# Retention and a gated feed-forward: the gates of 256 tokens by seven quarter products

## The chip, the cores and the metric

One core of one Trainium2 chip. The metric is device time in microseconds (us). The kernel works in bf16 with fp32 sums, on five engines: TensorE (PE), VectorE (DVE), ScalarE (ACT), GpSimd (POOL) and SyncE (SP, which issues DMAs). They run side by side and wait for each other by semaphores.

## The reference

```python
def _attn_ref(q, k, v):                       # (8, 8, 576, 64) each
    scores = scale * np.matmul(q, k.transpose(0, 1, 3, 2))
    gamma = 1.0 - 2.0 ** (-5.0 - np.arange(H))
    Dmat = np.where(rel >= 0, gamma[:, None, None] ** rel[None], 0.0)   # rel = pos_i - pos_j
    return np.matmul(scores * Dmat[None], v)

def _moe_ref(x, w_gate, w_val, w_out):        # x: 4608 tokens x 512; w: 512 x 1536, 1536 x 512
    gate = 1.0 / (1.0 + np.exp(-(x @ w_gate)))
    return (gate * (x @ w_val)) @ w_out
```

The tokens of the feed-forward are the retention's outputs, all heads of one position side by side.

## The kernel before

The retention is worked out in chunks of 64 positions with a running state, so that a "chunk group" makes, for two steps of 128 tokens, the masked scores (`row`), their products with v (`val`), the products with the old state, and the new state's share (`new`). The results stand transposed in `xT`, feature rows by token columns, which the feed-forward reads as the moving operand of its matmuls.

The feed-forward goes over the tokens in blocks: tokens 0 to 511, then `BLOCKS`: two blocks of 256 (512 and 768), then blocks of 512 from 1024 on. Of each block it makes the gates (`g`: products with `w_gate`, then a sigmoid on ACT), the values (`v`: products with `w_val`, multiplied into the gates on DVE, the result is `gv`), and the output products (`op`, with `w_out`).

The blocks of 512 tokens use seven products in the place of eight (Strassen's scheme in Winograd's form): a unit of four feature chunks by all 512 tokens is cut in quarters, and sums of quarters of the weights (`w_sums`, in `wgt_sb` for gates, `wvt` for values), of x (`xsum`) and of the products give the result. `quarter_units` makes one product at a time: `quarter("g", u, i)` is product i of gate unit u, short `gui`: g15 is product 5 of unit 1. Products 1, 6, 7 and 4 gather in the tile `gatea`, 5 and 3 in `gatee`, and 2 is added to a copy of `gatea` in `gateg`; ACT copies what is needed between (`gu`, `gs`), DVE adds, ACT takes the sigmoids. Before the change the two blocks of 256 tokens don't use this: `h_units` makes, for pairs of feature chunks, eight gate products and eight value products of 256 columns in turn (`h_g`, `h_v`), and `op_units` the output products.

There are eight PSUM banks: `tr`, `pv`, `st` one each, `qk` two, `ffn` three, used in a ring (`Ring`), so that a product's tile waits for the reader of the tile before it in its bank.

The order is written out by hand: each generator yields after a piece, and the loop over `BLOCKS` puts between the pieces what tables say. `SUMS_AT` has entries as 0.3:g00p: in block 0 of `BLOCKS` (tokens 512 to 767) at piece 3, sum 0 of gate unit 0 on POOL (p) or DVE (v); o are sums of `w_out` (`wt_sb`), w of the values' weights, c casts of the next chunks' inputs, t transposes on PE. `PAIRS_AT` says at which pieces the chunk groups of the next tokens stand. `CUTS` and `OP_CUTS` say how many 512-column products are made in two halves of 256 columns.

Of the kernel before, what the change touches and what calls it, by code (L numbers as in the profile page):

```python
# [9 lines left out]
FP32 = mybir.dt.float32  # L10
BF16 = mybir.dt.bfloat16
AF = mybir.ActivationFunctionType
ALU = mybir.AluOpType
# [3 lines left out]
def kernel(  # L17
# [19 lines left out]
    nc = tc.nc  # L37
# [4 lines left out]
    P = 128  # L42
    M = H // 2
    NC = (S + P - 1) // P
    NKC = DM // P
    NFC = DFF // P
# [43 lines left out]
    SUMS = 8  # L90
# [785 lines left out]
    def h_units(gvs, fcs, t0, n):  # L876

        for fc in fcs[::2]:
            gv_tile(gvs, t0, fc)
            both = made[t0, fc // 4][:, fc % 4:fc % 4 + 2, 0:n]  # L880
            for what, w_sb in (("g", wg_sb), ("v", wv_sb)):
# [9 lines left out]
                yield 8 * n  # L891

    def gv_unit(t0, u):

        return gv_pool.tile([P, 4, 512], BF16, tag="gv", name=f"gv_{t0}_{u}")
# [91 lines left out]

    def first_x_sum(i, eng):

        if 0 not in turned_x:  # L990
            turned_x[0] = [ld_pool.tile([P, 2, 2, 256], BF16, tag="xsum", name=f"xsum_0_{i}", bufs=SLOTS["xsum"])
                           for i in range(2)]
        t1, t2, t3, t4 = (turned_x[0][i][:, j] for i in range(2) for j in range(2))
        b11, b12, b21, b22 = (xT(slice(r, r + 2), slice(c, c + 256)) for r in (0, 2) for c in (0, 256))
        to, a, b = ((t1, b12, b11), (t3, b22, b12), (t2, b22, t1), (t4, b21, t2))[i]
        eng.tensor_tensor(out=to, in0=a, in1=b, op=ALU.subtract)
# [4 lines left out]

    def quarter_units(gvs, t0):

        BANKS = {("g", 0): [(tr_psum, "tr"), (pv_psum, "pv"), (qk_psum, "qk")],
                 ("g", 1): [(qk_psum, "qk"), (ffn_psum, "ffn"), (st_psum, "st")],
                 ("g", 2): [(pv_psum, "pv"), (st_psum, "st"), (st_psum, "st") if thirds(t0) else (tr_psum, "tr")],
                 ("w", 0): [(ffn_psum, "ffn"), (qk_psum, "qk"), (ffn_psum, "ffn")],
                 ("w", 1): [(ffn_psum, "ffn"), (ffn_psum, "ffn"), (ffn_psum, "ffn")],
                 ("w", 2): [(qk_psum, "qk"), (qk_psum, "qk"), (tr_psum, "tr")]}
        waiting = []  # L1010

# [3 lines left out]

        def bank(kind, u, i):
# [3 lines left out]
            return pool.tile([P, 2, 256], FP32, tag=tag, name=f"{name}_{t0}_{u}", **more)  # L1020

        def keep(kind, u, name, ps, eng=on_act):
            t = sum_tile([P, 2, 256], FP32, f"{kind}{name}_{t0}_{u}")
            eng(out=t, in_=ps)
            return t

        def right(i):
            x = xT(ALL, slice(t0, t0 + 512))
            t = turned_x[t0] if i > 3 else None
            return {1: lambda: x[:, 0:2, 0:256], 2: lambda: x[:, 2:4, 0:256], 3: lambda: x[:, 2:4, 256:512],  # L1030
                    4: lambda: t[1][:, 1], 5: lambda: t[0][:, 0], 6: lambda: t[0][:, 1], 7: lambda: t[1][:, 0]}[i]()

# [18 lines left out]
        def quarter(kind, u, i, by=nc.gpsimd):  # L1051

            me = of.setdefault((kind, u), {})
            if i == 1:
                gv_tile(gvs, t0, 4 * u)
                me["a"] = bank(kind, u, 0)
            if i == 5:
                me["e"] = bank(kind, u, 2)
            a, e = me.get("a"), me.get("e")
            product(kind, u, i, {1: a, 6: a, 7: a, 4: a, 5: e, 3: e, 2: me.get("g")}[i], i in (1, 5))  # L1060
            behind_copy = i in (1, 5) and (t0 == BLOCKS[2][0] and i == 1 or (kind, u) == ("w", 0))
            if not behind_copy and (kind, u, i) != ("g", 1, 5):
                settle()

            def leaves(r, h, src, eng=nc.vector, parts=1):
                for n in range(parts):
                    part = slice(2 * n // parts, 2 * (n + 1) // parts)
                    to = made[t0, u][:, 2 * r:2 * r + 2, h * 256:(h + 1) * 256][:, part]
                    if kind == "g":
                        nc.scalar.activation(out=to, in_=src[:, part], func=AF.Sigmoid)  # L1070
                    else:
                        eng.tensor_tensor(out=to, in0=to, in1=src[:, part], op=ALU.mult)  # L1072

            if i == 1:
                me["g"] = bank(kind, u, 1)
                nc.scalar.copy(out=me["g"], in_=a)  # L1076
            elif i == 2:
                leaves(0, 0, me["g"])
            elif i == 5:
                me["s5"] = keep(kind, u, "s5", e, on_dve if t0 == BLOCKS[2][0] and (kind, u) in KEEP_DVE else on_act)  # L1080
            elif i == 6:
                me["u2"] = keep(kind, u, "u2", a)
            elif i == 3:
                nc.vector.tensor_tensor(out=me["u2"], in0=e, in1=me["u2"], op=ALU.add)  # L1084
# [8 lines left out]
            return 4 * 256  # L1093

        H_CUTS = 4

        def value(fc):
# [13 lines left out]
            return 4 * 512  # L1111

        return quarter, value

# [180 lines left out]

    OP_CUTS = (6, 11, 0, 0)

# [59 lines left out]

    CUTS = 60
    cut = []
# [110 lines left out]
    for i in range(2):  # L1470
        first_x_sum(i, nc.vector)
    first_sum(sbd[3], "share_1", on_act)
# [16 lines left out]

    step(units, 1)  # L1490
    first_x_sum(2, nc.vector)
    step(units, 1)
    first_x_sum(3, nc.vector)
    step(units, 2)
# [46 lines left out]
    def op_first(fcs, nbs, opps):  # L1541
        for fc in fcs:
            for nb in nbs:
# [51 lines left out]

    SUMS_AT = ("0.0:c03p 0.1:f00p 0.3:g00p 0.3:w10v 0.3:w11v 0.6:t01p 0.7:o10p 0.8:c02v "
# [3 lines left out]
               "2.22:o02p 2.39:o12v 3.2:w20v 3.2:w21v 3.3:w23v 3.9:w22v").split()  # L1600
    sums_at = {}
    for x in SUMS_AT:
# [5 lines left out]
            w_sums(k, i, u, eng))  # L1608
    PAIRS_AT = ((0, 10), (0, 11), (1, 10), (1, 0))
    paired = 0  # L1610
# [4 lines left out]
    for w, (t0, n) in enumerate(BLOCKS):  # L1615
# [13 lines left out]
        while w > 1 and (not twos and valued < last or twos and twos[-1][0][-1] < last):  # L1629
            vals = list(range((twos[-1][0][-1] if twos else valued) + 1, at))  # L1630
            twos.append((vals, list(range(at, min(at + 2, NS)))))
            at = min(at + 2, NS)
        for i, cols in enumerate(ffn_units(t0, n, nxt)):
            for x in sums_at.get((w, i), ()):
                x()
# [20 lines left out]
        assert not twos  # L1656
        assert w != 1 or paired == len(PAIRS_AT)
        while len(pending) > (w == 1):
            pending.pop(0)()
# [31 lines left out]
```

## Time and profile before

| | |
|---|---|
| median of 3 runs | 303.66 us (303.56 to 304.35) |
| the profiled execution | 303.61 us |
| its span, first instruction to last | 302.0 us |
| PE busy | 295.4 us (98%), 4430 matmuls recorded |
| DVE, ACT, POOL busy | 230.1, 204.6, 224.9 us (76%, 68%, 74%) |
| granted TensorE clock | 1.0 |

The times of the trace count from the start of the span; the 1.6 us between span and run lie outside it. A row of the timeline has start, length and instruction, with xN where N alike follow each other; the length of a row of matmuls includes the way of the last one through the array, so paces are read from start to start. A few matmul records are missing.

### The profile page before, as it was taken

Reading aid. Unit: us, or ns where it says so; the run is one execution under the profiler, and the core shown is the slowest. Engines: PE = TensorE matmul, PEld = TensorE weight load, DVE = VectorE, ACT = ScalarE, POOL = GpSimd, SP = SyncE. Lnnn points to the kernel's source line nnn. Section 1 sums busy time; section 2 is a strip of 40 time slices with the busy share of each in tenths; the row PEclk is TensorE's granted clock in tenths of the full one; section 3 lists DMA queues with packets and bytes.
Section 4 is the critical chain, followed back from the end, with each engine's and each line's share of the span. In section 5 each row is a group of like instructions: output and inputs, shape, how many; then the busy total and the mean of one; then the engine's idle time right before and its main releaser. Section 6 shows DMA issues by size and latency. Waiting matters only on the chain.

```text
span 302.0 us, 10689 instructions
## 1 busy us (share of the span) xinstructions
PE 295.4 (98%) x4430; PEld 250.4 (83%) x4437; DVE 230.1 (76%) x439; ACT 204.6 (68%) x414; POOL 224.9 (74%) x253
## 2 busy tenths in 40 slices
PE   8999999999999999999999999999999999999994
PEld 3687876978868888888888888888888888888883
DVE  5967995686886998789748974896489848935793
ACT  6764574345369747985798589857985698559830
POOL 5775754846479898978997898789978947860780
PEclk9999999999999999999999999999999999999999
DMA  7999999979899979897759967976793165004013
GB/s 205 309 339 398 362 345 239 209 155 210 174 197 222 248 176 225 186 221 211 143 114 200 250 143 155 194 207 146 128 204 127 37 111 205 4 2 139 3 36 104
DMA packets 146464, 54.99 MB, mean 182 GB/s; under 512 B 124400, under 2 KB 139760, under 8 KB 146416
## 3 DMA queue, kind: packets, MB, share of 16 engines
q1 hardware_dynamic: 145328, 53.59, 73.3%
q10 hardware_dynamic: 1088, 0.72, 0.8%
q8 instruction: 34, 0.56, 0.8%
q14 instruction: 14, 0.11, 0.1%
HBM read 37.75 MB, written 9.44 MB: 156 GB/s over the span
## 4 chain that ended last, share of the span: by engine, by line
PE 86%; DMA 7%; SPq 4%; POOL 1%; issue 0%; ACT 0%; DVE 0%
PE gatea L1045 12%; PE wa L1045 12%; PE qa L1172 11%; PE qe L1172 9%; PE gatee L1045 6%; PE we L1045 6%; PE h_v L885 4%; PE h_g L885 3%; PE op L1305 3%; DMA wv<-in_moe_w_val_dram 3%; PE op L1548 3%; PE gateg L1045 3%; PE wg L1045 3%; SPq L186 3%; DMA wg<-in_moe_w_gate_dram 2%; PE val L717 2%
## 5 line engine op out<-in xcount | busy, mean ns | idle before, releaser
L1045 PEld LDWEIGHTS <-wg_sb 128*128 128x128 bf16 x348 | 34.0, 98 | 4.2
L1072 POOL TENSOR_TENSOR gv<-gv,wu 128x512 bf16<-128x512 bf16 x20 | 23.5, 1174 | 16.1 <-DVE wu L1084 16.0
L1172 PEld LDWEIGHTS <-gsum 128*128 128x128 bf16 x312 | 29.9, 98 | 3.7
L1045 PEld LDWEIGHTS <-wv_sb 128*128 128x128 bf16 x296 | 29.0, 98 | 3.4
L429 POOL TENSOR_TENSOR qk<-q,qtab 128x512 bf16<-128x512 f32 x28 | 30.1, 1073 | 1.4 <-DMA q<-in_q_dram 1.4
L1084 DVE TENSOR_TENSOR gu<-gatee,gu 128x512 f32<-128x512 f32 x22 | 15.2, 690 | 19.4 <-ACT gateg L1076 10.2
L1045 PEld LDWEIGHTS <-wgt_sb 128*128 128x128 bf16 x264 | 25.8, 98 | 3.0
L942 POOL TENSOR_TENSOR gsum<-gsum,gv 128x256 bf16<-128x256 bf16 (+1 forms) x20 | 17.6, 891 | 14.4 <-DVE gsum L942 12.6
L1045 PE MATMUL gatea<-xsum,wg_sb 128*128 128x256 bf16 x172 | 25.6, 273 | 0.0
L1172 PEld LDWEIGHTS <-gv 128*128 128x128 bf16 x228 | 21.8, 98 | 2.7
L429 POOL TENSOR_TENSOR qk<-k,ktab 128x512 bf16<-128x512 f32 x11 | 12.1, 1097 | 13.9 <-DMA k<-in_k_dram 9.6
L1087 DVE TENSOR_TENSOR gs<-gatea,gs 128x512 f32<-128x512 f32 x22 | 15.1, 688 | 9.4 <-PE gatea L1045 9.3
L942 POOL TENSOR_TENSOR gsum<-gv,gsum 128x256 bf16<-128x256 bf16 (+1 forms) x24 | 21.9, 921 | 0.2
L703 DVE TENSOR_TENSOR pt<-row,tri 128x512 bf16<-128x512 f32 x30 | 19.2, 681 | 2.9 <-PE row L686 2.7
L442 POOL TENSOR_TENSOR v<-v,ktab 128x512 bf16<-128x512 f32 x19 | 20.9, 1100 | 0.0
L1045 PE MATMUL wa<-xsum,wv_sb 128*128 128x256 bf16 x136 | 20.4, 273 | 0.0
L658 ACT CAST sb<-s 128x512 bf16<-128x512 f32 (+1 forms) x26 | 14.3, 569 | 8.4 <-DVE s L828 8.3
L787 ACT CAST xT<-val 128x512 bf16<-128x512 f32 x26 | 14.7, 592 | 7.0 <-PE val L733 7.0
L942 DVE TENSOR_TENSOR gsum<-gv 128x512 bf16<-128x512 bf16 (+1 forms) x34 | 18.7, 576 | 0.0
L1045 PEld LDWEIGHTS <-wvt 128*128 128x128 bf16 x168 | 16.4, 98 | 1.9
L942 POOL TENSOR_TENSOR gsum<-gv 128x256 bf16<-128x256 bf16 (+1 forms) x20 | 17.6, 880 | 0.0
L1070 ACT ACTIVATE gv<-gu 128x512 bf16<-128x512 f32 x22 | 14.0, 638 | 5.2 <-DVE gu L1084 5.2
(210 smaller groups left out, 882.6 us busy)
## 6 DMA issues: line engine op xcount, KB each, us to landing
k<-in_k_dram SPq DMA_DIRECT2D x26, 256.0 KB, 3.8
q<-in_q_dram SPq DMA_DIRECT2D x26, 256.0 KB, 4.2
v<-in_v_dram SPq DMA_DIRECT2D x26, 256.0 KB, 4.6
out_dram<-ob SPq DMA_DIRECT2D x24, 256.0 KB, 2.8
wg<-in_moe_w_gate_dram SPq DMA_DIRECT2D x12, 256.0 KB, 5.3
wv<-in_moe_w_val_dram SPq DMA_DIRECT2D x12, 256.0 KB, 5.2
wo<-in_moe_w_out_dram SPq DMA_DIRECT2D x12, 256.0 KB, 5.3
v32p<-in_v_dram SPq DMA_DIRECT2D x6, 256.0 KB, 4.7
```

Source lines behind the costliest of these rows:

```text
L429: eng.tensor_tensor(out=to, in0=by_halves(loaded[s][1 - i]), in1=tab, op=ALU.mult)
L442: nc.gpsimd.tensor_tensor(out=natural["v", s], in0=loaded[s][2], in1=tab, op=ALU.mult)
L658: eng(out=both_steps["sb", b, c][:, js], in_=both_steps["s32", b, c][:, js])
L703: nc.vector.tensor_tensor(out=t[:, y, 0:n].rearrange("p i m t -> p (i m) t"), in0=rows_tile[ss[0]][y][:, 0:n].rearrange("p i m t -> p (i m ...
L787: nc.scalar.copy(out=to, in_=src)
L885: nc.tensor.matmul(ps[:, i], lhsT=w_sb[:, kc, (fc + i) * P:(fc + i + 1) * P], rhs=xT(kc, slice(t0, t0 + n)), start=(kc == 0), stop=(kc == ...
L942: eng.tensor_tensor(out=to, in0=a, in1=b, op=op)
L1045: nc.tensor.matmul(ps[:, f], lhsT=w[:, kc, f * P:(f + 1) * P], rhs=x[:, kc], start=(first and f == 0 and kc == 0), stop=(f == 1 and kc == ...
L1072: eng.tensor_tensor(out=to, in0=to, in1=src[:, part], op=ALU.mult)
L1084: nc.vector.tensor_tensor(out=me["u2"], in0=e, in1=me["u2"], op=ALU.add)
L1087: nc.vector.tensor_tensor(out=me["s5"], in0=a, in1=me["s5"], op=ALU.add)
L1172: nc.tensor.matmul(ps[:, b], lhsT=left(fp)[:, b * P:(b + 1) * P], rhs=right(fp), start=(first and fp == 0 and b == 0), stop=(fp == NFC // ...
```

## The change

The gates of tokens 768 to 1023 (the second block of 256) are made by seven quarter products of 128 columns each, as in the large blocks; the values stay plain products of 256 columns. `h_quarters` has the order of both in the table `SHORT`. Sums of x for that block are made by DVE ahead of it (`block_x_sum`). The sums of the gates' weights, which only tokens from 1024 on needed, are thus needed a block earlier and stand earlier in `SUMS_AT`: two go from POOL to DVE, two value sums from DVE to POOL. The chunk groups stand at other pieces. Halved products: 29 in place of 60 allowed in block 0 (48 were there), none in place of 17 in block 512's output products; matmuls in all stay at 4437.

```diff
+    SHORT = (("", "g01 g15 g11 v0", "g02 g05 g06 g16 g12", "g13 g03 g07 g17", "g21 v4 g04 g14 m", "v6 m m", "g26 v2 v8 g25", "g22", "m g27 g23", "V10", "m g24 m V11 m", ""),)
+
+    def h_quarters(gvs, t0, n):
+        quarter, _ = quarter_units(gvs, t0, n)
+        mults = []
+        for steps in SHORT[0]:
+            cols = 0
+            for x in steps.split():
+                if x == "m":
+                    quarter.settle()
+                    to, by = mults.pop(0)
+                    nc.vector.tensor_tensor(out=to, in0=to, in1=by, op=ALU.mult)
+                elif x[0] == "g":
+                    cols += quarter("g", int(x[1]), int(x[2]))
+                else:
...
+            yield cols
...
-    def first_x_sum(i, eng):
+    def block_x_sum(t0, n, i, eng):
...
-    def quarter_units(gvs, t0):
+    def quarter_units(gvs, t0, n=512):
+        m = n // 2
...
+        if n < 512:
+            BANKS["g", 0][2] = (st_psum, "st")
+            BANKS["g", 1][2] = (ffn_psum, "ffn")
...
-    OP_CUTS = (6, 11, 0, 0)
+    OP_CUTS = (0, 0, 0, 0)
...
-            yield from h_units(gvs, range(NFC), t0, n)
+            yield from h_quarters(gvs, t0, n) if t0 == BLOCKS[1][0] else h_units(gvs, range(NFC), t0, n)
...
-    CUTS = 60
+    CUTS = 29
...
-    SUMS_AT = ("0.0:c03p 0.1:f00p 0.3:g00p 0.3:w10v 0.3:w11v 0.6:t01p 0.7:o10p 0.8:c02v "
+    SUMS_AT = ("0.0:c03p 0.1:f00p 0.3:g00v 0.3:w10v 0.3:w11v 0.4:o10p 0.6:t01p 0.8:c02v 0.8:g01v 0.8:c05p "
...
-    PAIRS_AT = ((0, 10), (0, 11), (1, 10), (1, 0))
+    PAIRS_AT = ((0, 8), (0, 13), (1, 10), (1, 2))
...
+        X_SHORT = ('vvvv',)
+        if w == 1:
+            for i in range(4):
+                block_x_sum(t0, n, i, nc.vector if X_SHORT[0][i] == "v" else nc.gpsimd)
```

What this moves is seen at three places. The first is DVE behind the masks `pt` of the second chunk group of block 512 (`s` are the running states, `wt_sb` a sum of `w_out`, `h_v` the values of block 768). Before:

```order
L703 TENSOR_TENSOR pt_2_1619<-row_2_1_1536,tri_274 128x512
L830 COPY s32_2_0_1632<-new_2_0_1569 128x256
L828 TENSOR_TENSOR s32_2_0_1632<-s32_2_0_1632,new_2_1_1570 128x256
L828 TENSOR_TENSOR s32_2_1_1646<-s32_2_0_1632,new_2_0_1569 128x256
L828 TENSOR_TENSOR s32_2_1_1646<-s32_2_1_1646,new_2_1_1570 128x256
L324 TENSOR_TENSOR wt_sb_278<-wo_sb_277 128x512
L890 TENSOR_TENSOR gv_768_0_1661<-gv_768_0_1661,h_v_768_0_1673 128x2x256
```

And in the changed kernel, from the multiply of block 512's last values on:

```order
L890 TENSOR_TENSOR gv_512_2_1269<-gv_512_2_1269,h_v_512_10_1430 128x2x256
L365 TENSOR_TENSOR wg_sb_275<-wg_sb_275 128x2x256 x2
L703 TENSOR_TENSOR pt_2_1590<-row_2_0_1506,tri_274 128x512
L703 TENSOR_TENSOR pt_2_1590<-row_2_1_1507,tri_274 128x512
L830 COPY s32_2_0_1601<-new_2_0_1540 128x256
L828 TENSOR_TENSOR s32_2_0_1601<-s32_2_0_1601,new_2_1_1541 128x256
L365 TENSOR_TENSOR wg_sb_275<-wg_sb_275 128x2x256
L828 TENSOR_TENSOR s32_2_1_1613<-s32_2_0_1601,new_2_0_1540 128x256
L828 TENSOR_TENSOR s32_2_1_1613<-s32_2_1_1613,new_2_1_1541 128x256
L1023 TENSOR_TENSOR xsum_768_0_1628<-xT_768_1599 128x2x128
L1023 TENSOR_TENSOR xsum_768_1_1629<-xT_768_1599 128x2x128
```

Three gate sums (in place, in `wg_sb`) and the sums of x have come in; two more sums of x follow the last row shown, then the adds of the quarter products. The second place is ACT within the gates of block 768. Before:

```order
L888 ACTIVATE gv_0_1661<-h_g_0_1662 128x2x256
L888 ACTIVATE gv_0_1661<-h_g_2_1683 128x2x256
L888 ACTIVATE gv_1_1705<-h_g_4_1706 128x2x256
L888 ACTIVATE gv_1_1705<-h_g_6_1728 128x2x256
L888 ACTIVATE gv_2_1750<-h_g_8_1751 128x2x256
L888 ACTIVATE gv_2_1750<-h_g_10_1771 128x2x256
```

In the changed kernel, unit 2's part, which is the end of it:

```order
L1107 COPY gateg_2_1727<-gatea_2_1721 128x256
L1101 ACTIVATE gv_0_1634<-gatea_0_1635 128x2x128
L1101 ACTIVATE gv_1_1649<-gatea_1_1650 128x2x128
L1055 COPY gu_768_2_1766<-gatea_2_1721 128x256
L1055 COPY gs_768_2_1791<-gatee_2_1786 128x256
L1101 ACTIVATE gv_2_1720<-gateg_2_1727 128x2x128
L1101 ACTIVATE gv_2_1720<-gs_768_2_1791 128x2x128
L1101 ACTIVATE gv_2_1720<-gu_768_2_1766 128x2x128
L1101 ACTIVATE gv_2_1720<-gatea_2_1721 128x2x128
L787 CAST xT_2000<-val_0_1870 128x2x8x32
```

Six sigmoids have become nine copies and twelve sigmoids of half the width, and the last of them reads the bank that the next chunk group's `val` takes over. The third place is DVE in front of the first chunk group of block 512 (`T` is a turned input of that group):

```order
L890 TENSOR_TENSOR gv_512_0_1145<-gv_512_0_1145,h_v_512_2_1201 128x2x256
L365 TENSOR_TENSOR wgt_sb_279<-wg_sb_275 128x512
L365 TENSOR_TENSOR wvt_0_855<-wv_sb_276 128x512
L365 TENSOR_TENSOR wvt_1_856<-wvt_0_855,wv_sb_276 128x512
L890 TENSOR_TENSOR gv_512_1_1214<-gv_512_1_1214,h_v_512_4_1226 128x2x256
L632 COPY T_1_1246<-turn_1_1_1253 128x512
```

The gate sum in the second row is new here, where before the two `wvt` sums stood alone.

More of the change, by code (lines that the diff above doesn't have):

```diff
@@ L1014, in settle, with quarter_bank @@
                 waiting.pop(0)()
-        def bank(kind, u, i):
+        def quarter_bank(kind, u, i):
             pool, tag = BANKS[kind, u][i]
@@ L1065, in leaves @@
             def leaves(r, h, src, eng=nc.vector, parts=1):
-                for n in range(parts):
-                    part = slice(2 * n // parts, 2 * (n + 1) // parts)
-                    to = made[t0, u][:, 2 * r:2 * r + 2, h * 256:(h + 1) * 256][:, part]
+                for p in range(parts):
+                    part = slice(2 * p // parts, 2 * (p + 1) // parts)
+                    to = made[t0, u][:, 2 * r:2 * r + 2, h * m:(h + 1) * m][:, part]
                     if kind == "g":
@@ L1074, in quarter @@
             if i == 1:
-                me["g"] = bank(kind, u, 1)
+                me["g"] = quarter_bank(kind, u, 1)
                 nc.scalar.copy(out=me["g"], in_=a)
@@ L1092, in quarter @@
                 settle()
-            return 4 * 256
+            return 4 * m
         H_CUTS = 4
@@ L1111, in value @@
             return 4 * 512
+        quarter.settle = settle
         return quarter, value
@@ L1657 @@
         assert w != 1 or paired == len(PAIRS_AT)
+        assert not [x for x in sums_at if x[0] == w]
         while len(pending) > (w == 1):
```

47 lines of the change are left out of this document (29 added, 18 removed), and 3 rows, old and new, of the table SUMS_AT.

## The prediction

> **What bounds the kernel now.** I read the page first: its busy times, then the chain that ended last.
>
> ```profile
> PE 295.4 (98%) x4430; PEld 250.4 (83%) x4437; DVE 230.1 (76%) x439; ACT 204.6 (68%) x414; POOL 224.9 (74%) x253
> ...
> PE 86%; DMA 7%; SPq 4%; POOL 1%; issue 0%; ACT 0%; DVE 0%
> ```
>
> TensorE (PE) is the bound: 295.4 of 302.0 us, and 86% of the chain. Busy PE proves little where matmuls overlap, so I looked at starts. The timeline of PE, in the stretch that changes (start, us, instruction):
>
> ```profile
> 47.41 2.97 PE L1548 MATMUL op<-wo_sb,gv 128*128 128x512 bf16 x13 [0.16 <-issue]
> 50.21 0.61 PE L630 MATMUL turn<-ident,qk 128*128 128x128 bf16 x8
> ...
> 51.52 1.04 PE L885 MATMUL h_g<-xT,wg_sb 128*128 128x256 bf16 x8
> 52.40 1.04 PE L885 MATMUL h_v<-xT,wv_sb 128*128 128x256 bf16 x8
> 53.27 1.04 PE L885 MATMUL h_g<-xT,wg_sb 128*128 128x256 bf16 x8
> ...
> 57.64 0.61 PE L630 MATMUL turn<-ident,qk 128*128 128x128 bf16 x8
> 58.08 1.04 PE L885 MATMUL h_v<-xT,wv_sb 128*128 128x256 bf16 x8
> ```
>
> Start to start, eight products of 256 columns take 0.875 us (109 ns each), eight of 128 columns 0.44 to 0.45 (56 ns), thirteen of 512 columns 2.80 (215 ns). In all three the next group starts when the columns are through, and no other row of these stretches shows PE waiting. The later part of the same timeline:
>
> ```profile
> 65.90 0.32 PE L717 MATMUL val<-pt,v 64*64 64x64 bf16 x16
> ...
> 67.15 2.79 PE L1305 MATMUL op<-wo_sb,gv 128*128 128x512 bf16 x23
> 69.78 1.04 PE L885 MATMUL h_g<-xT,wg_sb 128*128 128x256 bf16 x8
> ...
> 79.50 0.34 PE L717 MATMUL val<-pt,v 64*64 64x64 bf16 x18
> ...
> 88.62 1.04 PE L1045 MATMUL gatea<-xT,wg_sb 128*128 128x256 bf16 x8
> ```
>
> A chunk group takes 1.25 us (65.90 to 67.15), and block 768's twelve groups fill 69.78 to 79.50 but for the last, with no idle time marked. So before has next to no PE wait here to remove: the change can win only columns, and loses whatever wait it makes.
>
> **PE's own work.** Removed: 48 gate products of 256 columns, 48 x 109 ns = 5.24 us. Added: 84 products of 128 columns (three units, seven products, four matmuls), 84 x 56 ns = 4.70 us. That is -0.54 us. Halving: 19 value and gate products in front and 17 output products of block 512 become whole; two halves are 2 x 109 = 218 ns, a whole one 215, so 36 x 3 ns = -0.11 us. The count of PE instructions stays equal (36 more, 36 fewer). Sum: **-0.65 us**.
>
> The eight turns each load their own weights, as the new products do; a load is listed longer than that pace:
>
> ```profile
> L630 PEld LDWEIGHTS <-qk 128*128 128x128 bf16 x24 | 1.6, 98 | 0.5
> ```
>
> 98 ns a load against 56 ns a product means that loads overlap each other, but eight in a row after long products is a short test, while the new gates run up to 36 in a row. I take 56 ns, the row of the same shape; the upper bound is a load's whole 98 ns, 84 x 42 = +3.5 us.
> The Trainium skill ("TensorE: Matmul & The Clock Gate", Back-to-back issue gap) speaks against this term: it states about 81 ns per matmul for a sustained stream of weight loads and 128-column matmuls, and 56 only for an isolated gap. By that figure the term would be 84 x 81 = 6.8 us, +1.56 instead of -0.54, an estimate; the trace's eight at 56 ns disagree as far as they go.
>
> **VectorE in front of the gates.** Quarter products need sums of x before the second of them (g15), so VectorE (DVE), free of it before, now stands in PE's way. Its rows after the chunk group at 65.90, and what a bf16 sum costs:
>
> ```profile
> 55.89 0.42 DVE L365 TENSOR_TENSOR wvt<-wv_sb 128x512 bf16<-128x512 bf16 x1
> 56.34 1.15 DVE L365 TENSOR_TENSOR wvt<-wvt,wv_sb 128x512 bf16<-128x512 bf16 x1
> 57.41 0.68 DVE L890 TENSOR_TENSOR gv<-gv,h_v 128x512 bf16<-128x512 bf16 x1
> ...
> 66.86 1.29 DVE L703 TENSOR_TENSOR pt<-row,tri 128x512 bf16<-128x512 f32 x2 [0.37 <-PE row L686]
> 68.06 0.41 DVE L830 COPY s<-new 128x256 f32<-128x256 f32 x1
> 68.51 1.40 DVE L828 TENSOR_TENSOR s<-s,new 128x256 f32<-128x256 f32 x3
> ```
>
> GpSimd (POOL) beside them:
>
> ```profile
> 56.09 1.12 POOL L429 TENSOR_TENSOR qk<-k,ktab 128x512 bf16<-128x512 f32 x1 [0.24 <-DMA k<-in_k_dram]
> ...
> 58.91 1.15 POOL L365 TENSOR_TENSOR wgt_sb<-wg_sb 128x512 bf16<-128x512 bf16 x1
> ...
> 68.67 1.04 POOL L429 TENSOR_TENSOR qk<-k,ktab 128x512 bf16<-128x512 f32 x1 [4.77 <-DMA k<-in_k_dram]
> 69.68 1.04 POOL L429 TENSOR_TENSOR qk<-q,qtab 128x512 bf16<-128x512 f32 x1
> ```
>
> The sum at 56.34 took 1.15 instead of 0.42 and ended at 57.49, just behind POOL's product, which ended at 57.21: a DVE sum of two SBUF tensors stands still while POOL works. The Trainium skill ("SBUF — State Buffer", SBUF: two separate sides) has this as an exclusive lock on a port pair that the two share, held for a whole instruction; the trace agrees (1.15 against 0.42 us), and the rule speaks against adding such sums to DVE.
>
> Let C be the start of the chunk group in front of block 768's gates. PE: 1.25 us of chunks, then 16 whole output products, 16 x 0.215 = 3.45, first gate product at C+4.70, g15 four products later at C+4.92. DVE: masks from C+0.96 (66.86 - 65.90), state sums until C+4.01 (68.51 + 1.40 = 69.91), one weight sum between them (0.42, or 1.15 beside POOL), then the first x sum of 256 columns, nearest row:
>
> ```profile
> L942 DVE TENSOR_TENSOR gsum<-gv 128x256 bf16<-128x256 bf16 x12 | 3.5, 333 | 0.0
> ```
>
> So the sum is there at C+4.01+0.42+0.33 = C+4.76 at best, and with POOL's products at 68.67 and 69.68 in the way at up to C+4.01+1.15+0.9 = C+6.0. In front of the masks DVE now also has h_v_10's multiply and two gate sums, 0.68 + 2 x 0.42 = 1.5 us that came earlier or later before. PE's wait: 0 to 1.1 us; I take **+0.4**, since the group and POOL's casts fall near each other.
> Farther in front, one gate sum (0.42 to 1.15 us) is queued ahead of h_v_4's multiply, which frees the bank of h_g_8. That multiply ended at 58.09 (57.41 + 0.68) and h_g_8 follows h_v_6 at 58.95, so 0.86 us covers it: a wait of 0 to 0.3. One output-weight sum comes ahead of the state that the second chunk group reads, at worst the 0.73 by which a stuck sum is longer than a free one. Both need POOL at the wrong moment: **+0.1**.
>
> **ScalarE within the gates.** Six sigmoids of 512 columns become nine copies and twelve sigmoids of 256. Rows by form, and the delay from PE:
>
> ```profile
> L888 ACT ACTIVATE gv<-h_g 128x512 bf16<-128x512 f32 x12 | 7.2, 597 | 11.6 <-PE h_g L885 11.6
> ...
> L1236 ACT COPY ob<-qa 128x256 f32<-128x256 f32 x12 | 3.9, 376 | 2.7 <-PE qa L1172 2.7
> ...
> L1444 ACT ACTIVATE gv<-hg 128x256 bf16<-128x256 f32 x4 | 1.4, 384 | 1.4 <-PE hg L1438 1.4
> ...
> 52.60 0.60 ACT L888 ACTIVATE gv<-h_g 128x512 bf16<-128x512 f32 x1 [0.29 <-PE h_g L885]
> ```
>
> That is 9 x 0.376 + 12 x 0.384 = 8.0 us for 3.6, in some 10 us of PE time: ScalarE (ACT) keeps up on average, so what counts is each turnaround. ACT starts 0.20 us after PE goes on (52.60 - 52.40), so a copy is done 0.58 us after its product. From unit 2's fifth product to its third lie two products of 4 x 56 ns, 0.45 us: a wait of 0.13. The last sigmoid frees the bank that the next chunk group writes first; between its product and that group lies one value product of 4 x 109 = 0.44 us against 0.20 + 0.384, and a VectorE sum of 0.33 with its sigmoid is queued before it: 0.1 to 0.3. Together 0 to 0.6, taken **+0.3**. The v2 and v8 products wait for multiplies of v0 and v4 on DVE, which two output-weight sums now precede; POOL mostly waits for loads there, so 0, at worst 0.5.
>
> **Moved for nothing.** Two gate sums leave POOL (1.15 us each, row at 58.91), and one value sum comes to it early; its casts there start by the loads (4.77 us of waiting at 68.67), so neither shortens nor delays them. A last value sum goes from DVE to POOL in block 1536, where POOL has this room:
>
> ```profile
> POOL gv L1072 <- DVE wu L1084: 16.0, 7, 7.1
> ```
>
> Without it, it would cost up to the 1.15. Earlier casts issue their loads and transposes on SyncE in the same order as before.
>
> **Sum:** -0.65 + 0.4 + 0.1 + 0.3 = +0.15 us on the profiled execution's 303.61 (span 302.0 and 1.6 around it), 303.8 us. The median of the three runs is 303.66, so the same to 0.05.
>
> **Rivals.** (A) No wait survives: the turnarounds overlap, DVE has its sums in time. Then 303.61 - 0.65 = 303.0. For it: DVE is idle a quarter of the span. Against: C+4.76 for C+4.92 leaves 0.16. (B) DVE becomes the bound ahead of the gates: each of the weight sums falls beside a POOL product, and g15 waits 1.1 us, h_g_8 and the chunk state 0.8 of their 1.0, with 0.3 behind: 303.61 - 0.65 + 2.2 = 305.2; half of the port losses give 304.5. It decides as slower once these waits pass 0.65 + 0.9 = 1.55 us. For it: seven more bf16 sums on DVE between 53 and 71 us. Against: POOL stood idle from 63.9 to 68.67. (C) The new products don't hold 56 ns, since a load of 98 ns shows through: up to 303.8 + 3.5 = 307.3. The product rows speak against it. By the sustained 81 ns of the Trainium skill ("TensorE: Matmul & The Clock Gate", Back-to-back issue gap) it would be 303.8 + 84 x 25 ns = 305.9, again an estimate. (D) The halved products were worth more than 3 ns each as fillers; 36 of them made whole move every later instruction by less than 0.11 us, so no case of its own.
>
> **How the numbers follow.** A measurement of this kernel can tell about 0.3%, 0.9 us, from no change: 302.75 to 304.57. Forecast 0.50 (0.47 within, 0.03 slower), A 0.20 (0.16 within, 0.04 faster, as it would need more than PE's columns), B 0.24 (0.22 slower, 0.02 within), C 0.06 slower. Faster 0.04, same 0.65, slower 0.31. The range goes from A's 303.0 less 0.1 to B's 305.2.
>
> **What would show it.** In the profile after: h_g's 48 rows for block 768 gone, 84 of 128 columns at 56 ns start to start (C: 80 or more); a gap on PE ahead of g15, released by VectorE's x sum (0.4; A: none; B: over 1), a gap of 0.1 to 0.2 ahead of unit 2's third product by ACT, and one ahead of the chunk group behind. Block 1024's first gate product starts at 88.62 before; in after it should stand within 0.2 us later, and everything behind it as before. If the time changes behind block 1024 instead, the whole account is wrong.

## The result, and the profile after

| | before | after |
|---|---|---|
| median | 303.52 us (14 runs, 303.07 to 304.35) | 304.50 us (14 runs, 303.49 to 305.78) |
| ratio after to before, 95% interval | | 1.0031 (1.0015 to 1.0046) |
| the profiled execution, its span | 303.61, 302.0 us | 304.73, 303.0 us |

The change costs 0.98 us. That is at the edge of what the forecast called the same (304.57), inside its range, and 0.7 above its value. The page of the changed kernel, busy times and chain:

```profile
PE 295.5 (98%) x4428; PEld 247.3 (82%) x4437; DVE 237.7 (78%) x450; ACT 208.0 (69%) x429; POOL 226.0 (75%) x253
...
PE 90%; DVE 6%; ACT 1%; issue 1%; DVEq 0%
```

VectorE has 7.6 us more work, ScalarE 3.4, and VectorE stands on the chain with 6% where it had none. The count of weight loads is the same, 4437. The timeline of PE in the changed kernel, at the places that the prediction spoke of and at those that it didn't:

```profile
60.90 1.04 PE L885 MATMUL h_g<-xT,wg_sb 128*128 128x256 bf16 x8
62.35 1.03 PE L885 MATMUL h_v<-xT,wv_sb 128*128 128x256 bf16 x8 [0.41 <-DVE gv L890]
...
69.91 0.39 PE L1076 MATMUL gatea<-xT,wg_sb 128*128 128x128 bf16 x4
70.14 0.39 PE L1076 MATMUL gatee<-xsum,wgt_sb 128*128 128x128 bf16 x4
70.36 0.39 PE L1076 MATMUL gatea<-xT,wg_sb 128*128 128x128 bf16 x4
...
72.16 0.61 PE L1076 MATMUL gatea<-xsum,wgt_sb 128*128 128x128 bf16 x8
...
74.81 0.61 PE L1076 MATMUL gatea<-xsum,wg_sb 128*128 128x128 bf16 x8
75.26 1.04 PE L913 MATMUL h_v<-xT,wv_sb 128*128 128x256 bf16 x8
...
78.68 0.39 PE L1076 MATMUL gatea<-xsum,wg_sb 128*128 128x128 bf16 x4
79.08 0.38 PE L1076 MATMUL gatee<-xT,wgt_sb 128*128 128x128 bf16 x4
...
80.70 0.34 PE L717 MATMUL val<-pt,v 64*64 64x64 bf16 x18
...
89.13 1.04 PE L1076 MATMUL gatea<-xT,wg_sb 128*128 128x256 bf16 x8
90.53 0.60 PE L1076 MATMUL gatee<-xsum,wgt_sb 128*128 128x256 bf16 x4 [0.36 <-DVE xsum L995]
```

Start to start is what to read. 60.90 to 62.35 is 1.45 for eight products of 256 columns that need 0.875: PE waits 0.58 ahead of h_v_10. 74.81 to 75.26 is eight products of 128 columns: 56 ns each. 69.91, 70.14, 70.36 are 0.22 to 0.23 apart, four products each: g15, the second row, waits for nothing. 78.68 to 79.08 is 0.40 in the place of 0.22: 0.18 of waiting. 89.13 to 90.53 is 1.40 for eight products that need 0.875: 0.53 of waiting, where the kernel before went on from 88.62 without one:

```profile
89.50 0.60 PE L1045 MATMUL gatee<-xsum,wgt_sb 128*128 128x256 bf16 x4
```

Counted from block 512's first h_g, which takes the loads in front out of the comparison, three stretches (us):

| from | to | before | after | waits found in after | columns |
|---|---|---|---|---|---|
| first h_g | block 768's first gate | 18.25 | 18.94 | 0.58 ahead of h_v_10; 0.17 in the chunk group at 65.04 | -0.05 to -0.11 |
| there | block 1024's first gate | 18.85 | 19.21 | 0.25 ahead of g06, 0.13 of v8, 0.18 of g23, 0.21 and 0.13 at the chunk group | -0.54 |
| there | first output product of block 1024 (`qa`) | 18.77 | 19.52 | 0.53 ahead of block 1024's second gate product, 0.19 at 97.74 | 0 |

Waits of 2.37 us less 0.6 of columns are 1.77, and the stretch grew by 1.80. From the first `qa` to the last product the kernel before takes 190.3 us and the changed one 190.2. The two spans differ by less, 1.0, since this execution's h_g began 0.54 earlier (50.98 for 51.52; over all traces it lies between 50.60 and 53.30) and what follows the last product was 0.2 shorter. Three more traces below have the same sums and gates as the changed kernel (unedited once more, with the halves back, with idle products in front); their stretches to the first `qa` are 57.54, 57.24 and 56.87 us, so beside the 55.87 of before the loss is 1.0 to 1.8 us, and this trace shows the most of it.

Who held PE up, VectorE first (start, length, instruction), then GpSimd, then ScalarE, in the same execution:

```profile
59.29 1.22 DVE L365 TENSOR_TENSOR wgt_sb<-wgt_sb,wg_sb 128x512 bf16<-128x512 bf16 x1
60.43 1.27 DVE L703 TENSOR_TENSOR pt<-row,tri 128x512 bf16<-128x512 f32 x2
61.63 0.67 DVE L890 TENSOR_TENSOR gv<-gv,h_v 128x512 bf16<-128x512 bf16 x1
...
69.69 1.37 DVE L1023 TENSOR_TENSOR xsum<-xT 128x256 bf16<-128x256 bf16 x2
70.98 1.74 DVE L1023 TENSOR_TENSOR xsum<-xT,xsum 128x256 bf16<-128x256 bf16 x2
...
87.50 0.67 DVE L365 TENSOR_TENSOR wv_sb<-wv_sb 128x512 bf16<-128x512 bf16 x1
88.09 1.26 DVE L324 TENSOR_TENSOR wt_sb<-wo_sb,wt_sb 128x512 bf16<-128x512 bf16 x1
...
90.05 0.75 DVE L995 TENSOR_TENSOR xsum<-xT 128x512 bf16<-128x512 bf16 x2
```

```profile
59.07 1.15 POOL L324 TENSOR_TENSOR wt_sb<-wo_sb 128x512 bf16<-128x512 bf16 x1
...
69.86 1.04 POOL L429 TENSOR_TENSOR qk<-k,ktab 128x512 bf16<-128x512 f32 x1 [4.78 <-DMA k<-in_k_dram]
70.86 1.09 POOL L429 TENSOR_TENSOR qk<-q,qtab 128x512 bf16<-128x512 f32 x1
...
87.84 1.22 POOL L429 TENSOR_TENSOR qk<-q,qtab 128x512 bf16<-128x512 f32 x1
```

```profile
78.66 0.37 ACT L1055 COPY gs<-gatee 128x256 f32<-128x256 f32 x1 [1.73 <-PE gatee L1076]
...
80.28 0.37 ACT L1101 ACTIVATE gv<-gatea 128x256 bf16<-128x256 f32 x1
```

The gate sum at 59.29 took 1.22, and GpSimd's sum beside it went from 59.07 to 60.22; the masks and the multiply of h_v_8 stood behind it, and h_v_10 needs the bank that this multiply frees at 62.30. The second pair of x sums took 1.74 beside GpSimd's two products; its first sum ended at 72.10, and g06 began at 72.16. The sum at 88.09 took 1.26 beside GpSimd's product at 87.84. ScalarE's copy ended at 79.03 and the product that waited for it, g23, began at 79.08; its last sigmoid ended at 80.65 and the chunk group began at 80.70.

### The profile page after: what moved, and what is told of

The parts are those of the page before. It is cut to its first block, busy times and chain, and to the rows that moved or that the text cites. A ratio compares the mean times of both kernels' runs of the same rounds, so it can differ in the third digit from the quotient of the medians.

```text
span 303.0 us, 10714 instructions
## 1 busy us (share of the span) xinstructions
PE 295.5 (98%) x4428; PEld 247.3 (82%) x4437; DVE 237.7 (78%) x450; ACT 208.0 (69%) x429; POOL 226.0 (75%) x253
## 4 chain that ended last, share of the span: by engine, by line
PE 90%; DVE 6%; ACT 1%; issue 1%; DVEq 0%
PE gatea L1076 13%; PE wa L1076 12%; PE qa L1204 11%; PE qe L1204 9%; PE gatee L1076 7%; PE we L1076 6%; PE op L1580 3%; PE gateg L1076 3%; PE wg L1076 3%; PE hv L1405 3%; PE qa L1280 2%; PE hg L1405 2%; PE val L717 2%; PE idle L242 2%; PE val L733 1%; PE row L686 1%
## 5 line engine op out<-in xcount | busy, mean ns | idle before, releaser
L1076 PEld LDWEIGHTS <-wg_sb 128*128 128x128 bf16 x396 | 37.2, 98 | 4.8
L1115 DVE TENSOR_TENSOR gu<-gatee,gu 128x512 f32<-128x512 f32 (+1 forms) x25 | 16.4, 658 | 20.1 <-ACT gateg L1107 9.6
L1076 PEld LDWEIGHTS <-wgt_sb 128*128 128x128 bf16 x300 | 28.3, 98 | 4.3 <-issue 0.7
L1076 PE MATMUL gatea<-xsum,wg_sb 128*128 128x256 bf16 (+1 forms) x196 | 27.6, 266 | 0.0
L1118 DVE TENSOR_TENSOR gs<-gatea,gs 128x512 f32<-128x512 f32 (+1 forms) x25 | 16.3, 657 | 9.0 <-PE gatea L1076 9.0
L1101 ACT ACTIVATE gv<-gu 128x512 bf16<-128x512 f32 (+1 forms) x25 | 15.2, 611 | 5.3 <-DVE gu L1115 5.3
L1101 ACT ACTIVATE gv<-gs 128x512 bf16<-128x512 f32 (+1 forms) x25 | 15.1, 607 | 5.3 <-DVE gs L1118 5.3
```

The costliest lines, as they stand in the source:

```text
L1076: nc.tensor.matmul(ps[:, f], lhsT=w[:, kc, f * P:(f + 1) * P], rhs=x[:, kc], start=(first and f == 0 and kc == 0), stop=(f == 1 and kc == ...
```

## The experiments

Times are medians over rounds in turn with the kernel before on the same chip, and ratios are to it; its median lay between 303.52 and 303.73, so differences from the changed kernel's 304.50, which was measured at another time, are good to some 0.2 us. A "hole" is a place where PE is held up and the profile names no engine or load as the releaser; its size is taken from start to start less the columns, which is 0.15 to 0.2 more than the idle time that the row marks issue. Rows marked issue where only the record of a matmul is missing are not counted. Counted in the traces is the number of the weight load, from 0, at which a hole ends.

**The halved products put back.** Edit to the changed kernel:

```diff
-    CUTS = 29
+    CUTS = 60
-    OP_CUTS = (0, 0, 0, 0)
+    OP_CUTS = (6, 11, 0, 0)
```

> The change with the 36 halved products put back in front (19 in block 0, 17 in block 512's output), all else as in the changed kernel. Theory V (the loss is PE waiting for VectorE, whose sums of two SBUF tensors stand still while GpSimd works): 36 x 3 ns = +0.1 us of PE, partly inside waits, so within 0.3 us of the changed kernel, near +0.3% of the kernel before. Rival H (the halves filled waits, or their count set where the later instructions lie): 0.5 to 1 us faster than the changed kernel, back at the time of before.

Measured: 308.43 us (307.35 to 309.08), ratio 1.0158 (1.0134 to 1.0181): 3.9 us over the changed kernel, for 36 products that cost 3 ns each by their columns. No expectation had that. Its timeline of PE, far behind the edit:

```profile
144.99 1.36 PE L1204 MATMUL qe<-wt_sb,gsum 128*128 128x256 bf16 x11 [0.72 <-issue]
149.27 0.22 PE L733 MATMUL val<-T,sb 64*64 64x64 bf16 x3 [1.63 <-issue]
182.18 0.49 PE L1204 MATMUL qa<-wo_sb,gsum 128*128 128x256 bf16 x3 [1.27 <-issue]
```

The holes stand inside runs of one product, and no engine or load releases them. The first ends at weight load 2143, the others at 2271 and 2783, 128 and 5 x 128 later. A table of the page has the queue that may belong to this (packets, MB, share); first of this kernel, then of before:

```profile
q8 instruction: 35, 0.57, 0.8%
```

```profile
q8 instruction: 34, 0.56, 0.8%
```

Each packet carries 16,384 bytes. With 4,437 pairs of load and product, 34 packets are one for each 128 pairs: pages of 256 instructions.

**Plain gates in the changed schedule.** Block 768 gets `h_units` back, without its x sums; three gate sums that are made in place go behind their last reader.

```diff
-            yield from h_quarters(gvs, t0, n) if t0 == BLOCKS[1][0] else h_units(gvs, range(NFC), t0, n)
+            yield from h_units(gvs, range(NFC), t0, n)
...
-0.11:g12v 0.11:g02v ... 0.15:g22v ... 1.5:o03v 1.6:c04p
+1.5:g02v 1.5:o03v 1.6:g12v 1.6:c04p ... 2.1:g22v
```

> The moved sums, chunk groups and whole products of the change, but the gates of tokens 768 to 1023 plain again (products of 256 columns, no sums of x), with the three sums in place in wg_sb back behind that block. Theory V: the wait of h_v_10 on VectorE in front of the second chunk group (0.58 us in the changed kernel) stays, since the sums queued ahead of it stay; the waits within the gates go; PE pays 0.54 us more columns: about the time of before plus 0.2 to 0.7 us. Rival Q (the quarter products' own turnarounds between ScalarE and VectorE are the loss): h_v_10 hardly counts, the time is that of before within 0.2 us. Rival G (the new places of the chunk groups are the loss): as slow as the changed kernel or slower, +1 us.

Measured: 305.41 us (305.00 to 307.06), ratio 1.0076 (1.0050 to 1.0102). This has 36 products fewer, and its trace has holes of 0.46 and 0.48 us at weight loads 3039 and 3679, so it says nothing clean about the gates. No expectation had 1.8 us over before; the wait ahead of h_v_10 is 0.14 here, not the 0.58 that theory V kept. The next run is cleaner.

**The same, with the 36 halves in front,** so that the count of PE's instructions is that of before.

```diff
 (the edit above, and)
+    CUTS = 60
+    OP_CUTS = (6, 11, 0, 0)
```

> The changed kernel's new places of the sums and of the groups of chunks, with the twelve plain gate products of before in block 768 and with the 36 halved products back in front, so that TensorE's instruction count is again that of before everywhere. Theory 1 (the loss is in the schedule: sums on VectorE that stand still beside GpSimd's work, in front of block 768 and of block 1024): +0.7 to +1.1 us against before, 304.3 to 304.7, with a wait of 0.5 to 0.95 ahead of block 1024's second gate product. Theory 2 (the loss is in the quarter products: their x sums, their turnarounds on ScalarE): within 0.3 of before, 303.4 to 303.9. On instruction fetch: if the plain gates with 36 fewer products lost 0.46 us at 203 us and 0.48 at 238 because the instructions stood at other places in their 16 KB pages, both holes are gone here; if not, they stay.

Measured: 304.41 us (303.12 to 305.59), ratio 1.0026 (1.0008 to 1.0044). Both holes are gone, and theory 1's time came out: the new places of the sums and of the chunk groups cost 0.84 us with before's own gate products. No run parts the sums from the chunk groups. Its timeline of PE, where the waits are for VectorE:

```profile
58.87 1.03 PE L885 MATMUL h_g<-xT,wg_sb 128*128 128x256 bf16 x8 [0.53 <-DVE gv L890]
62.55 1.03 PE L885 MATMUL h_v<-xT,wv_sb 128*128 128x256 bf16 x8 [0.15 <-DVE gv L890]
...
90.93 0.60 PE L1076 MATMUL gatee<-xsum,wgt_sb 128*128 128x256 bf16 x4 [1.13 <-DVE xsum L995]
```

Start to start less the columns, PE waits 0.69 ahead of h_g_8 (58.87), 0.32 ahead of h_v_10 (62.55) and 1.29 ahead of block 1024's second gate product (90.93), for which 0.5 to 0.95 had been expected.

Quarter products on top (304.50) change the median by 0.1. The table above says why that may be: their 0.54 of columns stand against 0.90 of waits, most of them turnarounds, in which a product waits for another engine to copy, add or multiply what an earlier one left.

**Four sums moved into GpSimd's wait for loads.**

```diff
-... 0.4:o10p 0.6:t01p 0.8:c02v ... 0.9:o00v ... 0.11:g12v 0.11:g02v ...
+... 0.6:t01p 0.7:c04p 0.7:o10p 0.7:o00p 0.7:g02p 0.7:g12p 0.8:c02v ...
```

> The changed kernel with four sums (two of w_out, two in place in wg_sb) on GpSimd behind the cast of step 4, where it waits 4.8 us for a load; one of them came before that cast, one to three stood on VectorE. Theory V: VectorE's gate sum at 59.3 (1.22 us beside GpSimd's sum) takes 0.42, the w_out sum at 62.2 (1.27) is gone, so the waits ahead of h_v_10 (0.58), the output products (0.22) and the second x sum (0.25) go or halve: 0.6 to 1.0 us faster than the changed kernel. Rivals Q and G: these waits only move to the gates behind, within 0.3 us of the changed kernel.

Measured: 304.61 us (303.72 to 305.43), ratio 1.0031 (1.0016 to 1.0047). In its trace the wait ahead of h_v_10 fell from 0.58 to 0.14 and block 1024's first gate came 0.37 earlier; but the wait ahead of the second grew from 0.53 to 0.76. No gain in time, where theory V had 0.6 to 1.0.

**The end of the gates and the start of block 1024.** Order t1, t2, t3, t4 of block 768's x sums, one more look on ScalarE, and the last output sum of the table behind block 1024's x sums in the place of ahead of them.

```diff
-        to, a, b = ((t1, b12, b11), (t3, b22, b12), (t2, b22, t1), (t4, b21, t2))[i]
+        sums = (t1, b12, b11), (t3, b22, b12), (t2, b22, t1), (t4, b21, t2)
+        to, a, b = sums[(0, 2, 1, 3)[i] if t0 else i]
...
-    LOOK_ACT = (0, 5,
+    LOOK_ACT = (0, 2, 5,
...
-1.15:w02v 1.16:o23v 2.3:o22v
+1.15:w02v 2.1:o23v 2.3:o22v
```

> The changed kernel with three small moves behind the front: the x sums of block 768 in the order that the products need them (second and third swapped), the glance at the first chunk group's values on ScalarE instead of behind VectorE's three multiplies, and one w_out sum moved from ahead of block 1024's x sums into block 1024. Theory V: the waits of g06 (0.25), of the chunk group's last products (0.20) and of block 1024's first sum (0.53) go or halve: 0.4 to 0.9 us faster than the changed kernel. Rival Q: only the first counts, 0.1 to 0.3 us faster. If front waits alone set the time, no difference.

Measured: 304.31 us (303.93 to 306.05), ratio 1.0028 (1.0010 to 1.0046). VectorE in its trace, where block 1024's x sums now follow one weight sum and not two:

```profile
89.03 0.68 DVE L365 TENSOR_TENSOR wv_sb<-wv_sb 128x512 bf16<-128x512 bf16 x1
...
90.42 0.75 DVE L995 TENSOR_TENSOR xsum<-xT 128x512 bf16<-128x512 bf16 x2
91.09 0.42 DVE L995 TENSOR_TENSOR xsum<-xT,xsum 128x512 bf16<-128x512 bf16 x1
91.42 0.42 DVE L324 TENSOR_TENSOR wt_sb<-wo_sb,wt_sb 128x512 bf16<-128x512 bf16 x1
```

Its two gate rows stand at 90.73 and 91.60, 0.87 apart: that wait is gone, g06's too, and the stretch to the first `qa` is 0.9 shorter than the changed kernel's. The median fell by only 0.2, where theory V had 0.4 to 0.9.

**Both fixes together,** the four sums on GpSimd and the three edits above (the order of x sums is that of block 768, not of block 1024 as the expectation has it).

> The changed kernel with four sums moved into GpSimd's wait for loads in front (two of gates, two of output weights), block 1024's x sums in the order t1, t2, t3, t4, one more look on ScalarE, and the last output sum of block 1024 at step 2.1. Theory 1 (the waits in front of block 768 and of block 1024 are the loss, and each edit removes its own): block 512's first h_g to block 1152's first output product 56.3 to 56.6 us (changed kernel 57.67, before 55.87), time 303.5 to 304.0, which is still not under before, since the 0.6 us of turnarounds within the gates stay. Theory 2 (what is won in front is lost again behind): 304.3 to 304.6.

Measured: 303.91 us (302.94 to 305.22), ratio 1.0011 (0.9995 to 1.0027), stretch 56.70: somewhat over theory 1's 56.3 to 56.6, its time as expected. So removing these waits together brings back 0.6 of the 0.98 in the medians, and 0.97 of the 1.80 in the traces, though the intervals of the two ratios overlap and neither fix showed it alone. It doesn't beat before; the turnarounds of 0.18 and 0.21 are still there, and two holes:

```profile
85.87 0.32 PE L694 MATMUL new<-v,qk 64*64 64x64 bf16 x15 [0.30 <-issue]
...
118.34 0.49 PE L1205 MATMUL qe<-wo_sb,gsum 128*128 128x256 bf16 x3 [0.16 <-issue]
```

**One output sum moved on GpSimd alone.**

```diff
-... 0.4:o10p 0.6:t01p ... 0.9:o00v 0.9:c07p
+... 0.6:t01p ... 0.9:o00v 0.9:o10p 0.9:c07p
```

> The changed kernel with one sum of output weights on GpSimd moved from step 0.4 to 0.9, so that it stands behind the casts of chunks 4 and 5 and not beside VectorE's gate sum; VectorE's order is untouched. Theory 1 (the gate sum, 1.22 us instead of 0.42, stands still beside GpSimd's sum and puts off the multiply of h_v_8, for which h_v_10 waits): the gate sum takes 0.42, the wait of 0.58 us ahead of h_v_10 shrinks to 0 to 0.1, block 1024's first gate product stands 0.4 to 0.6 us earlier, counted from block 512's first h_g; 304.0. Theory 2 (h_v_10 waits for something else, or GpSimd's casts take the sum's place beside it): the wait stays at 0.4 or more, 304.5.

Measured: 304.83 us (304.24 to 305.83), ratio 1.0039 (1.0019 to 1.0058). Its gate sum, and its holes:

```profile
58.91 0.42 DVE L365 TENSOR_TENSOR wgt_sb<-wgt_sb,wg_sb 128x512 bf16<-128x512 bf16 x1
```

```profile
80.92 0.31 PE L694 MATMUL new<-v,qk 64*64 64x64 bf16 x15 [0.23 <-issue]
...
86.30 0.31 PE L694 MATMUL new<-v,qk 64*64 64x64 bf16 x15 [0.96 <-issue]
```

VectorE's order is untouched, yet the sum takes 0.42 in the place of 1.22, h_v_10 waits 0.14 in the place of 0.58, and block 768's first gate comes 0.41 earlier, as theory 1's mechanism has it; but the unedited kernel's second trace, below, has the same 0.42 and 0.14, so this trace alone doesn't show that the edit did it. The time did not follow: at weight loads 1119 and 1247 there are holes of 0.39 and 1.14 us, at the same instructions where the changed kernel's first trace had none.

**The kernel before with its halved products whole, and nothing else.**

> The kernel before with the 36 halved products whole and nothing else: 36 fewer TensorE products in front, so all later instructions stand 72 places earlier. Theory 1 (halving costs 3 ns a product, place in the pages does not matter): 303.4 to 303.6, no hole. Theory 2 (the place in the instruction pages matters): two or three holes of 0.3 to 0.8 us, marked issue, inside runs of one product and 1.3 to 1.5 us behind the landing of a 16 KB fetch, near 201 and 236 us as in the plain gates; 304.2 to 305.0.

Measured: 305.17 us (303.70 to 306.56), ratio 1.0047 (1.0021 to 1.0074): theory 2, 1.6 us for taking 36 products away. The traced execution was its fastest and has one hole, of 0.30 at weight load 3039, the place of one in the plain gates.

**The same with 36 products more at the start.** Five idle products of 512 columns become 41 of 64.

```diff
-    FILLS = (0, 0, 10)
+    FILLS = (0, 0, 5)
+    for _ in range(41):
+        nc.tensor.matmul(idle[-1][:, 0, 0:64], lhsT=blank, rhs=blank[:, 0:64], start=True, stop=True)
```

> The kernel before with its 36 halved products whole (which took 305.17 us), and at its very start five of the ten idle products of 512 columns replaced by 41 of 64 columns, so that TensorE has as many instructions as the kernel before, and from the halved products on each stands at the place it had there. Theory 1 (the places of the 16 KB instruction pages were the loss; in the traces so far every hole marked issue stands at weight load 95 of a group of 128): back to 303.3 to 303.7, no hole over 0.2 us. Theory 2 (the whole products themselves, or the ends of work on other engines, were the loss): 304.8 to 305.4.

Measured: 303.52 us (302.81 to 305.48), ratio 1.0003 (0.9982 to 1.0024), no hole. The 1.6 us are back, by products that compute nothing. That holes made up the 1.6 us is argued, since the one trace of the unpadded kernel, its fastest execution, shows 0.30 of them.

**The changed kernel with the same edit.**

> The changed kernel with nothing but 36 more idle products at its start (41 of 64 columns for five of 512), all later instructions as they are, 36 weight loads later in their pages: the places of the kernel with the halved products put back, which took 308.4 us. Theory 1 (places of pages): 307 to 309, holes of 0.8 to 1.8 us at weight loads 2143, 2271 and 2783 counted from 0, near 145, 149 and 182 us. Theory 2 (the halved products did it, not the places): 304.3 to 304.8.

Measured: 307.25 us (306.78 to 308.26), ratio 1.0121 (1.0094 to 1.0148): 2.75 us over the changed kernel. Its holes:

```profile
147.76 0.22 PE L735 MATMUL val<-T,sb 64*64 64x64 bf16 x3 [0.88 <-issue]
...
180.34 0.49 PE L1206 MATMUL qa<-wo_sb,gsum 128*128 128x256 bf16 x3 [0.97 <-issue]
```

They are at weight loads 2271 and 2783, as with the halves back; the one at 2143 did not come. Its two holes, 1.05 and 1.14 us, are what it takes longer from the first `qa` on (192.4 us for 190.2). With the two kernels ahead this shows that the number of PE instructions in front, and by these holes their place in the pages, is worth 1.6 us to the one kernel and 2.75 to the other.

**Both fixes with 8 products more at the start.**

> The kernel with both fixes (303.91 us; its trace has holes of 0.48 and 0.33 us at page ends) with 8 more TensorE products at its start (9 of 64 columns for one of 512), which by its trace lengthens the shortest stretches between page ends from 2.7 to 3.0 us. Theory 1 (page places still cost it some 0.5 us): 303.3 to 303.6, and with that at or under the kernel before. Theory 2 (what holes it has come by chance from run to run): 303.8 to 304.1.

Measured: 305.35 us (303.99 to 308.37), ratio 1.0053 (1.0027 to 1.0080). Both theories fell: 1.4 us worse, with holes of 0.68 and 0.75 us at weight loads 1247 and 1759. The shortest stretch between page ends doesn't tell how a place will do.

**The changed kernel once more.**

> The changed kernel once more, nothing edited: one more trace of it, to tell which waits are the program's and which the run's. Theory 1 (the waits for VectorE are the program's): 0.3 to 0.7 us ahead of h_v_10 and 0.3 to 1.0 ahead of block 1024's second gate product again, 0.18 and 0.31 at unit 2's third product and at the chunk group, while holes at weight loads 1119 and 1247, which the trace of the one moved output sum had and the changed kernel's first trace had not, come or stay away by chance. Theory 2 (the waits are the run's): the first two are gone or elsewhere.

Measured: 305.24 us, one run. Its timeline of PE, VectorE's gate sum and GpSimd's sum:

```profile
77.53 1.03 PE L913 MATMUL h_v<-xT,wv_sb 128*128 128x256 bf16 x8 [0.22 <-DVE gv L905]
86.70 0.32 PE L694 MATMUL new<-v,qk 64*64 64x64 bf16 x15 [0.30 <-issue]
90.94 0.60 PE L1076 MATMUL gatee<-xsum,wgt_sb 128*128 128x256 bf16 x4 [0.22 <-DVE xsum L995]
...
59.83 0.42 DVE L365 TENSOR_TENSOR wgt_sb<-wgt_sb,wg_sb 128x512 bf16<-128x512 bf16 x1
...
58.51 1.15 POOL L324 TENSOR_TENSOR wt_sb<-wo_sb 128x512 bf16<-128x512 bf16 x1
```

Half of theory 1: the waits at block 1024 (0.39), at g23 (0.18) and at the chunk group (0.21) are the program's. A wait of 0.10 ahead of g15 is the run's, for the first trace had none: GpSimd's product began ahead of the first x sum here, and that sum took 0.91 in the place of 0.29. The one ahead of h_v_10 is the run's too: GpSimd's sum ended at 59.66, just ahead of VectorE's at 59.83, and PE waited 0.14. So is the hole at weight load 1247, 0.48 here. Others came for them (v8 0.38 for 0.13), and the stretch to the first `qa` is again long, 57.54.

## Why the prediction was nearly right

**PE's columns (-0.65)** held. 128-column products keep 56 ns among the gates (32 in a row from 72.16 to 73.94), so rival C fell; of the 98 ns of a load nothing shows. The sustained 81 ns of the Trainium skill ("TensorE: Matmul & The Clock Gate", Back-to-back issue gap) do not appear in runs of this length. The halves' -0.11 is too small to be told from nothing (303.52 whole and padded).

**VectorE in front (+0.4 for g15, +0.1 farther ahead)** was right in kind and wrong in place. g15 waited 0 and g06 0.25. The first x sum ended at 69.97, 0.17 ahead of g15: it had begun just before GpSimd's product at 69.86, and that was luck, since in the second trace it stood still and g15 waited 0.10. Farther ahead, "both need POOL at the wrong moment: +0.1" is the mis-sized term: 0.75 in the first trace, 0.2 in the second. The wait ahead of h_g_8, put at 0 to 0.3, is in neither of them, but was 0.37 with the halves back and with the padding and 0.69 with plain gates and halves. The prediction followed the stuck sum to h_g_8 and to the chunk group's state, and not on through the masks to h_v_8's multiply and the bank of h_v_10.

**ScalarE (+0.3)**: g23 0.18 for 0.13, the chunk group 0.21 for 0.1 to 0.3, v8 0.13 for 0. It was right, with another 0.13 at the end of that chunk group, whose last products wait for a VectorE row queued behind three multiplies.

**"Moved for nothing"** is the step that failed. It looked only at sums that changed engine. A value sum that stayed on VectorE moved from 1.7 to 1.15, ahead of block 1024's x sums, beside an output sum that stood there already. In before only one sum stands between the masks and these:

```profile
87.00 0.41 DVE L324 TENSOR_TENSOR wt_sb<-wo_sb,wt_sb 128x512 bf16<-128x512 bf16 x1
87.33 0.42 DVE L830 COPY s<-new 128x256 f32<-128x256 f32 x1
...
88.11 0.98 DVE L969 TENSOR_TENSOR xsum<-xT 128x512 bf16<-128x512 bf16 x2
```

In after there are two, of 0.67 and 1.26: 0.53 of waiting in the first trace, 0.39 in the second, 1.29 with plain gates and halves, none with the output sum moved away. "Everything behind it as before", said of block 1024's first gate product, was wrong by 0.75 in the first trace and 0.6 in the second; that product itself stood 1.05 later, counted from block 512's first h_g, and not within 0.2. The prediction had called its whole account wrong if the time changed behind block 1024 instead. It changed on both sides: the waits in front were foreseen in kind, the one behind was not. Of waits the sum had 0.8 us; the first trace has 2.37: 0.75 in front, 0.25 for g06, 0.65 by ScalarE's turnarounds and the two beside them, and 0.72 from block 1024's first gate product on.

**The rivals.** A fell, since waits survived. B named the mechanism that decided, sums that stand still beside GpSimd, and its half-way price of 304.5 is what came; but its waits stood at g15, h_g_8 and the chunk state, with 0 at the first two in the first trace, so that the sizes meet is chance. D was left without a case with the words that whole products "move every later instruction by less than 0.11 us". In the change that holds, since 36 loads go and 36 come, though the sum used this as a count only; where an experiment broke the equality it was off by up to 3.9 us.

What stays open: two traces of the changed kernel have 1.7 to 1.8 us more to the first `qa` while the medians differ by 1.0. On the profiled execution of before, 1.8 us more would have been 305.4, beyond the range's 305.2; so that the time lies inside the range is in part luck. With waits and holes that come and go, one or two traces of a kernel can't settle the rest.

## What to carry to other kernels

Follow every moved instruction of an engine that feeds the bound, also those that stay on it, up to the next thing that waits for it; a list of what changed engine isn't enough. Before a difference of one per cent is put down to an edit, compare the number of instructions ahead of the dense parts: one run padded with idle products tells whether it matters, though not which padding will be good. Smaller products win columns, and give them back at each turnaround through another engine that is longer than the product behind which it hides.

## What the hardware showed

**Instruction pages.** Behind the first 20 us, the 14 traces have 15 holes of over 0.3 us. All end at a weight load whose number leaves 95 when divided by 128, 1.2 to 1.55 us after a packet of 16,384 bytes landed on the instruction queue. Some of them, and the largest of before (0.18):

| kernel | ends at us | weight load | PE held up, us | since the packet landed, us |
|---|---|---|---|---|
| before | 230.97 | 3551 = 27 x 128 + 95 | 0.18 | 1.65 |
| halves back | 149.27 | 2271 = 17 x 128 + 95 | 1.79 | 1.39 |
| halves back | 182.18 | 2783 = 21 x 128 + 95 | 1.44 | 1.32 |
| one output sum moved | 86.30 | 1247 = 9 x 128 + 95 | 1.14 | 1.39 |
| plain gates | 238.06 | 3679 = 28 x 128 + 95 | 0.48 | 1.54 |
| both fixes, 8 more | 119.34 | 1759 = 13 x 128 + 95 | 0.75 | 1.41 |

There are as many packets as such places (34, or 35 with 36 products more). Call the weight loads 95, 223, 351 and so on crossings, and what lies between two of them a page. A fetch started between 1.7 us before a crossing and 3.9 after it and took 0.9 to 2.5 us. All 15 holes came 3.3 to 5.4 us after the crossing ahead of them, in pages with chunk groups (94 to 118 of their 128 products have 64 columns); most pages as short had no hole, and where the page lasted 9.5 us or more, none of the weight loads at a crossing came over 0.22 us after the one before it. This suggests that a page that is through quickly can ask for the next before it is there. What sets the start of a fetch isn't known, and so not which place will be good. The Trainium skill ("Runtime: NRT & Kernel Launch", Instruction fetch mechanics) has the refill in blocks of 16 KiB, as here, and calls the cost of crossing a boundary "mostly hidden"; in this kernel it was up to 1.8 us at one crossing.

**A stuck sum.** A VectorE sum of two bf16 tensors of 512 columns took 0.42 us alone and up to 1.40 beside GpSimd's work (95.03 in the trace of the end of the gates, beside a GpSimd sum from 95.00 on). Which it was could change from one run of the same program to the next: GpSimd's sum began 0.22 us ahead of the gate sum in one trace and 1.32 ahead in the other. The waits for loads in front of GpSimd's sums shift so much, hence a place beside GpSimd that is free in one trace isn't free for good.
